# Attention and feed-forward on one core: the first two query blocks with queries on partitions, weights in half portions through a PSUM bank, and the opening's order in a table

## The chip, the cores and the metric

The kernel runs on one core of one Trainium2 chip. Five engines work side by side, each in the order of its own instructions, and wait for one another by semaphores: TensorE (PE, with its weight loads as PEld), VectorE (DVE), ScalarE (ACT), GpSimd (POOL) and SyncE (SP), which issues all transfers here. The metric is the device time of one execution in microseconds; lower is better.

## The reference

Block-causal attention of 8 batches with 8 heads, 576 positions and 64 features a head, then a feed-forward layer on the 4608 tokens. All of it is float32, and the feed-forward weights arrive as float64.

```python
scores = q @ k.T / sqrt(64)            # per batch and head
mask = (i // 64) >= (j // 64)          # a query block sees its own and earlier key blocks
attn = softmax(where(mask, scores, -1e9))
x = (attn @ v) laid out as [8 * 576, 512]
h = x @ w_in                           # 512 x 2048
out = (h * sigmoid(h)) @ w_out         # 2048 x 512
```

## The kernel before

**Tokens.** The queries of a head are treated in three ways. The first 64 (they see 64 keys) are done by `First`, four batches at a time, groups `a` and `b`. The second 64 (they see 128 keys) are done by `Second`, two batches at a time, groups `c1[0]` to `c1[3]`. The other 448 are done by `Unit`, one head at a time, 64 units in a loop. The feed-forward works on blocks of 256 tokens: blocks 0 and 1 are the tokens of `First`, blocks 2 and 3 those of `Second`, and 14 more come from the units.

**Products.** A *step* of a block covers two tiles of 128 hidden features. It has two products with `w_in` (`ffn1`, 12 matmuls each, L514) and, two steps later (`LAG`), two with `w_out` (`ffn2`, 6 matmuls each, L538). Between them stand `silu` (ScalarE, L521) and `split_g` (upper part on ScalarE, L526; lower part on GpSimd, L527). All operands are split in two float32r parts, whose products are added up. `ffn(n)` issues n products; there are 576 in all. Block 0 keeps its output in bank 2 and in the bank `U`, which the units need, so block 0 must be finished before the unit loop begins: 57 products are issued ahead of it. `EVEN` says how many steps blocks 0 and 1 take by turns. In the loop, `AHEAD` (152) is the number of products that are due when unit 17 starts; `pace` spreads them.

**Weights.** `Weights` turns float64 words into float32 in SBUF, 16 portions of two halves: `rebias` (ScalarE, L117), three bit steps on VectorE (L126, L130, L134), `his` (upper part, ScalarE, L144), `los` (lower part, GpSimd, L148). `weigh(k)` treats a whole portion, and its bit steps alternate between the halves. They read and write SBUF only.

**First and Second.** The scores stand with keys on partitions. A maximum over keys is therefore a 32-by-32 transposing reduction (`ttr`, L153), four copies (L454), four reductions and a transposing broadcast (`bcast`, L157); the sums go the same way. One exponential covers a bank of 512 columns (L378, L463). The normalization follows the product with `v`, and the tokens are split by `split_x` (ScalarE, L324; GpSimd, L325).

**Order.** Each engine runs its instructions in the order in which the code below writes them (`manual_schedule`): the opening is written out by hand from L625 to L685, then comes the loop over units. Transfers wait in SP's one queue, in the same order.

Of the kernel before, what the change touches and what calls it, by code (L numbers as in the profile page):

```python
# [56 lines left out]
def attn_ffn(ctx: ExitStack, tc: tile.TileContext, qk, v, qk0, v0, qk1, v1, w_in, w_out, out):  # L57
# [29 lines left out]
    class Weights:  # L87
        """Two ff tiles of w_in, or of w_out, in two halves."""

        def __init__(u, kind, d, raw, work):  # L90
            u.kind, u.d, u.tags, u.wtags = kind, d, raw, work
            if kind == "in":
                u.parts = [[w[:, 2 * i : 2 * i + 2, d * 256 : d * 256 + 256] for w in wi] for i in range(2)]
            else:
                u.parts = [[w[:, 2 * d + i, :] for w in wo] for i in range(2)]

        def load(u):
            """The float64 words."""
            u.raw = [
                T[:, :1024].bitcast(I64) if t == "T" else sp.tile([P, 512], I64, tag=t, name="wst", bufs=2 if t == "g2" else 1)  # L100
                for t in u.tags
            ]
            for i, st in enumerate(u.raw):
                if u.kind == "in":
                    src = w_in[2 * i * P : (2 * i + 2) * P, u.d * 256 : u.d * 256 + 256]
                    nc.sync.dma_start(out=st.rearrange("p (c f) -> p c f", c=2), in_=src.rearrange("(c p) f -> p c f", p=P))
                else:
                    f = 2 * u.d + i
                    nc.sync.dma_start(out=st, in_=w_out[f * P : f * P + P, :])
# [4 lines left out]
        def rebias(u):
            u.w = [sp.tile([P, 512], F32, tag=t, name="wm", bufs=2 if t == "ot" else 1) for t in u.wtags]
            for i in range(2):
                nc.scalar.activation(u.w[i], u.word(i, 1).bitcast(F32), AF.Copy, scale=REBIAS)  # L117

        def bits(u):
            """float32's bits, an instruction a step: exponent and upper fraction, sign, lower fraction.  # L120
            What lies under 2**-119 stays under it."""
            a = [z.bitcast(U32) for z in u.w]
            first = u.kind == "in" and u.d == 0  # its halves come one after the other
            for i, j in [(0, 0), (0, 1), (1, 0), (0, 2), (1, 1), (1, 2)] if first else [(i, j) for j in range(3) for i in range(2)]:
                if j == 0:
                    nc.vector.tensor_scalar(  # L126
                        out=a[i], in0=a[i], scalar1=3, scalar2=0x7FFFFFF8, op0=ALU.logical_shift_left, op1=ALU.bitwise_and
                    )
                elif j == 1:
                    nc.vector.scalar_tensor_tensor(  # L130
                        out=a[i], in0=u.word(i, 1), scalar=0x80000000, in1=a[i], op0=ALU.bitwise_and, op1=ALU.bitwise_or
                    )
                else:
                    nc.vector.scalar_tensor_tensor(  # L134
                        out=a[i], in0=u.word(i, 0), scalar=29, in1=a[i], op0=ALU.logical_shift_right, op1=ALU.bitwise_or
                    )
                yield
# [4 lines left out]
        def his(u):
            for i in range(2):
                nc.scalar.copy(u.parts[i][0], u.shaped(i))  # L144

        def los(u):
            for i in range(2):
                nc.gpsimd.tensor_tensor(out=u.parts[i][1], in0=u.shaped(i), in1=u.parts[i][0], op=ALU.subtract)  # L148

# [616 lines left out]
```

## Time and profile before

| | us |
|---|---|
| median of 3 runs | 1109.41 (1109.28 to 1111.64) |
| span of the profiled execution | 1107.8 |
| PE busy | 1047.5 (95%) |
| VectorE busy | 843.4 (76%) |
| ScalarE busy | 760.3 (69%) |
| GpSimd busy | 776.2 (70%) |

The span is the time from the first to the last instruction of the one execution that was profiled; its busy times are shares of that span over stages with different limits, so they say little by themselves. A row of the profile's groups reads: line, engine, operation, output and inputs by the program's names, shapes, count, then busy time, mean ns of one, and the idle time of the engine just before them with what ended it. The cut that matters here is by stage: the opening up to the loop's first scores, the first 17 units, and the rest.

### The profile page before, as it was taken

What the parts mean: (1) busy time and instruction counts of PE and PEld (TensorE: products, weight loads), DVE (VectorE), ACT (ScalarE), POOL (GpSimd) and SP (SyncE); (2) the same over time, 40 slices, a digit from 0 to 9 for tenths busy, and PEclk for the clock granted to TensorE, in tenths of its full rate; (3) what the DMA queues carried; (4) which work ended last, traced back from release to release, by engine and by line L of the source; (5) the groups of instructions that cost most, each with busy time, mean ns of one, the idle gap of its engine ahead of it and who ended that gap; (6) DMA issues with size and microseconds to landing.
All of it is one profiled execution on the core that took longest, in us unless ns stands there. A gap on an engine that the chain in (4) does not pass through costs nothing.

```text
span 1107.8 us, 19852 instructions
## 1 busy us (share of the span) xinstructions
PE 1047.5 (95%) x6848; PEld 941.5 (85%) x6848; DVE 843.4 (76%) x2504; ACT 760.3 (69%) x1222; POOL 776.2 (70%) x758
## 2 busy tenths in 40 slices
PE   4696789999999999999999999999999999999998
PEld 3585677888898999898999999999999898989997
DVE  6999995899999988888888888888888888810000
ACT  2454655888888787878787878778886878742221
POOL 1466558788888877878787878787787888642221
PEclk9798899999999999999999999999999999999999
DMA  7256522323223222212122212122322212000000
GB/s 247 91 172 186 156 88 64 91 54 79 66 68 78 56 69 71 70 51 70 51 71 68 76 51 70 51 71 59 76 60 51 70 51 79 23 20 20 1 20 19
DMA packets 44067, 79.92 MB, mean 72 GB/s; under 512 B 9152, under 2 KB 23488, under 8 KB 43968
## 3 DMA queue, kind: packets, MB, share of 16 engines
q1 hardware_dynamic: 43968, 78.66, 25.7%
q8 instruction: 54, 0.88, 0.4%
q14 instruction: 45, 0.37, 0.1%
HBM read 69.21 MB, written 9.44 MB: 71 GB/s over the span
## 4 chain that ended last, share of the span: by engine, by line
PE 69%; DVE 21%; ACT 3%; issue 3%; DMA 2%; POOL 1%; SPq 0%; POOLq 0%; DVEq 0%; ACTq 0%
PE o L538 28%; PE h L514 28%; PE U L294 6%; PE S L216 6%; DVE wm L130 2%; DVE Mx L153 2%; DVE Dx L153 2%; DVE wm L134 1%; DMA qk<-in_qk_dram 1%; DVE Xm L163 1%; DVE m L230 1%; DVE T L247 1%; DVE mb L157 1%; DVE X L482 1%; DVE Xd L163 1%
## 5 line engine op out<-in xcount | busy, mean ns | idle before, releaser
L514 PE MATMUL h<-x,wi 128*128 128x256 f32 x3456 | 448.9, 284 | 14.3 <-ACT x L324 11.8
L514 PEld LDWEIGHTS h<-x,wi 128*128 128x128 f32 x3456 | 432.3, 190 | 26.9 <-ACT x L324 12.1
L538 PE MATMUL o<-wo,g 128*128 128x512 f32 x1680 | 431.4, 401 | 2.1 <-ACT ot L545 2.1
L538 PEld LDWEIGHTS o<-wo,g 128*128 128x128 f32 x1680 | 305.2, 190 | 66.8 <-ACT ot L545 4.0
L267 POOL TENSOR_TENSOR pl<-p,ph 128x448 fp32r<-128x448 f32 (+1 forms) x192 | 225.5, 1204 | 107.8 <-ACT ph L260 107.8
L527 POOL TENSOR_TENSOR g<-g,g 128x512 fp32r<-128x512 f32 x144 | 186.8, 1297 | 115.7 <-ACT g L526 111.9
L153 DVE TRANSPOSE_TENSOR_REDUCE Mx<-S 64x4 f32<-64x128 f32 (+4 forms) x384 | 129.9, 401 | 94.8 <-PE S L216 94.6
L521 ACT ACTIVATE g<-h 128x512 f32<-128x512 f32 x144 | 86.0, 597 | 97.4 <-POOL g L527 56.1
L153 DVE TRANSPOSE_TENSOR_REDUCE Dx<-p 128x14 f32<-128x448 f32 (+3 forms) x320 | 123.3, 448 | 0.3 <-ACT p L255 0.3
L526 ACT CAST g<-g 128x512 fp32r<-128x512 f32 x144 | 89.4, 621 | 47.2 <-PE o L538 44.8
L193 POOL TENSOR_TENSOR qh<-qkraw,qh 64x576 fp32r<-64x576 f32 x64 | 101.4, 1584 | 6.8 <-ACT qh L189 2.1
L255 ACT ACTIVATE p<-T 128x512 f32<-128x512 f32 (+1 forms) x192 | 103.7, 603 | 0.7
L260 ACT CAST ph<-p 128x512 fp32r<-128x512 f32 (+1 forms) x192 | 101.9, 594 | 0.0
L294 PE MATMUL U<-ph,vc 128*128 128x448 f32 (+3 forms) x320 | 92.9, 303 | 1.7 <-ACT g L521 0.9
L216 PE MATMUL S<-qh 128*128 128x448 f32 (+3 forms) x320 | 92.7, 302 | 0.1
L521 ACT ACT_TABLE_LOAD x69 | 88.5, 1283 | 1.2
L255 ACT ACT_TABLE_LOAD x64 | 82.1, 1283 | 3.2 <-DVE T L245 2.0
L216 PE MATMUL S<-ql,qh 128*128 128x448 f32 (+3 forms) x320 | 84.0, 307 | 0.0
L294 PE MATMUL U<-pl,vc 128*128 128x448 f32 (+2 forms) x256 | 79.4, 332 | 0.5 <-POOL pl L267 0.5
L195 POOL TENSOR_TENSOR ql<-qkraw,qh 128x448 fp32r<-128x448 f32 x64 | 74.4, 1163 | 5.0
L247 DVE TENSOR_TENSOR T<-S,mb 128x256 f32<-128x256 f32 (+2 forms) x192 | 73.4, 409 | 0.0
L189 ACT CAST qh<-qkraw 128x1024 fp32r<-128x1024 f32 x64 | 66.9, 1046 | 3.8 <-DMA qkraw<-in_qk_dram 2.5
(89 smaller groups left out, 1229.7 us busy)
## 6 DMA issues: line engine op xcount, KB each, us to landing
qkraw<-in_qk_dram SPq DMA_DIRECT2D x128, 256.0 KB, 3.8
vraw<-in_v_dram SPq DMA_DIRECT2D x64, 160.0 KB, 2.7
wst<-in_moe_w_in_dram SPq DMA_DIRECT2D x15, 512.0 KB, 4.9
out_dram<-ot SPq DMA_DIRECT2D x24, 256.0 KB, 3.5
wst<-in_moe_w_out_dram SPq DMA_DIRECT2D x11, 512.0 KB, 3.7
qk<-in_qk_dram SPq DMA_DIRECT2D x16, 256.0 KB, 5.5
v<-in_v_dram SPq DMA_DIRECT2D x12, 256.0 KB, 4.8
out_dram<-ot SPq DMA_DIRECT2D x24, 128.0 KB, 3.2
```

What stands on the lines that cost most here:

```text
L153: nc.vector.tensor_reduce(out=out, in_=in_, axis=AX.X, op=op, apply_transpose=True)
L193: nc.gpsimd.tensor_tensor(out=u.qh[64:, NQ:], in0=u.raw[64:, NQ:], in1=u.qh[64:, NQ:], op=ALU.subtract)
L216: nc.tensor.matmul(u.ps(c, w, m), u.kk[:, j * P : j * P + m], qq[:, q0 : q0 + w], start=i == 0, stop=i == 1)
L255: nc.scalar.activation(u.p[:, c:e], T[:, c:e], AF.Exp, scale=SCALE)
L260: nc.scalar.copy(u.ph[:, c:e], u.p[:, c:e])
L267: nc.gpsimd.tensor_tensor(out=u.pl[:, c:e], in0=u.p[:, c:e], in1=u.ph[:, c:e], op=ALU.subtract)
L294: nc.tensor.matmul(U[:, q0 : q0 + w], u.vc[:, j, :], pp[:, c : c + w], start=n == 0, stop=n == 8)
L514: nc.tensor.matmul(h[:, f, :], wi[wt][:, c, w], x[:, xt, :], start=n == 0, stop=n == 3 * CT - 1)
L521: nc.scalar.activation(g, hs.pop((blk, d)), AF.Silu)
L526: nc.scalar.copy(g2[:, 0], g)
L527: nc.gpsimd.tensor_tensor(out=g2[:, 1], in0=g, in1=g2[:, 0], op=ALU.subtract)
L538: nc.tensor.matmul(o, g2[:, gt, f, tk], wo[wt][:, 2 * d + f, :], start=d == 0 and n == 0, stop=d == NSTEP - 1 and n == 5,)
```

## The change

**First and Second** now share a class `Early` and have the queries on partitions. The maximum is a plain reduction along the row (L360). Each head has its own exponential, in place in PSUM, with the negative maximum as bias and the row sum as second output (L369): eight of 64 columns, or four of 128. The weights are normalized before the product with `v` (`norm`, L377 to L380), turned by PE against an identity (`turn`, L386), copied back to SBUF (`back`, L389), and multiplied with `v`. Both parts of the tokens are made straight from PSUM, the upper on ScalarE, the lower on VectorE. A half of a `Second` group is one batch; both halves, and then the product with `v`, use bank 0 one after the other.

**Weights** come in 32 half portions, `w0` to `w31`, each with its own load. The first two bit steps write bank 1, and the third writes SBUF again (L152, L153, L156).

**The order** of the opening is a table of 350 entries: `a.`, `b.`, `c0.` to `c3.` and `w0.` to `w31.` with a method and a half, `ffn` (one product), `silu`, and `part` (`split_g`). The head before the loop has 61 products instead of 57, and `EVEN` is 6, with one step of block 0 ahead. The token tiles `x` become one tile with 16 parts. Units, loop and `AHEAD` stay as they were; the first unit is loaded behind the table.

```diff
-EVEN = 5
+EVEN = 6
+HEAD = 61
+ORDER = """
+a.load w0.load w1.load b.load a.load_v w0.rebias a.scores w2.load w3.load a.max:0 a.exp:0 a.max:1 w0.bits a.exp:1 b.scores w4.load
...
+b.norm:1 w3.rebias w3.bits ffn b.turn:0 w4.rebias
...
+w13.bits c1.turn:0 c1.back:0 w14.rebias ffn w12.hi w17.load c1.scores:1 c1.max:1 w13.hi c1.exp:1 ffn c2.load w12.lo w14.bits
...
+"""
-    xbuf = [cp.tile([P, 2, TB], F32R, name=f"x{i}") for i in range(NX)]
+    xbuf = cp.tile([P, NX, 2, TB], F32R, name="x")
...
         def bits(u):
+            w, a = u.w.bitcast(U32), bank(1).bitcast(U32)
+            nc.vector.tensor_scalar(out=a, in0=w, scalar1=3, scalar2=0x7FFFFFF8, op0=ALU.logical_shift_left, op1=ALU.bitwise_and)
+            nc.vector.scalar_tensor_tensor(
+                out=a, in0=u.word(1), scalar=0x80000000, in1=a, op0=ALU.bitwise_and, op1=ALU.bitwise_or
+            )
+            nc.vector.scalar_tensor_tensor(
+                out=w, in0=u.word(0), scalar=29, in1=a, op0=ALU.logical_shift_right, op1=ALU.bitwise_or
+            )
...
+    class Early:
+        def max(u, k):
+            n = 512 // u.KEYS
+            u.m[k] = sp.tile([P, 8], F32, tag=f"m{k}", name="m")[:, :n]
+            nc.vector.tensor_reduce(out=u.m[k], in_=u.ps[k].rearrange("p (h j) -> p h j", j=u.KEYS), axis=AX.X, op=ALU.max)
+            nc.vector.tensor_scalar(out=u.m[k], in0=u.m[k], scalar1=-SCALE, scalar2=None, op0=ALU.mult)
+        def exp(u, k):
...
+            for h in range(n):
+                nc.scalar.activation(
+                    heads[:, h], heads[:, h], AF.Exp, bias=u.m[k][:, h : h + 1], scale=SCALE, accum_out=u.rs[k][:, h : h + 1]
+                )
+        def norm(u, k):
...
+            nc.vector.tensor_scalar(out=u.rs[k], in0=u.rs[k], scalar1=1e-9, scalar2=None, op0=ALU.add)
+            nc.vector.reciprocal(out=rr, in_=u.rs[k])
...
+            nc.vector.tensor_tensor(out=out, in0=heads, in1=rr.unsqueeze(2).to_broadcast([P, n, u.KEYS]), op=ALU.mult)
+        def turn(u, k):
+            p = u.p[k]
+            for c in range(CT):
+                s = slice(P * c, P * c + P)
+                nc.tensor.transpose(u.ps[k][:, s], p[:, s], ident)
+        def back(u, k):
+            nc.scalar.copy(u.p[k], u.ps[k])
...
+    class Second(Early):
...
+        def scores(u, k):
...
+            u.ps[k] = bank(0)
...
+        def hi(u):
+            x = u.tiles(2 + u.g // 2, P)
+            u.xs = [x[:, :, i, P * (u.g % 2) : P * (u.g % 2) + P] for i in range(2)]
+            nc.scalar.copy(u.xs[0], u.x.rearrange("p (c q) -> p c q", c=CT))
+        def lo(u):
+            nc.vector.tensor_tensor(out=u.xs[1], in0=u.x.rearrange("p (c q) -> p c q", c=CT), in1=u.xs[0], op=ALU.subtract)
...
-    steps = [(blk, d) for d in range(EVEN) for blk in range(2)]
+    steps = [(0, 0)] + [z for d in range(EVEN) for z in ((0, d + 1), (1, d))]
...
+    for token in ORDER.split():
+        name, _, method = token.partition(".")
+        if method:
+            method, _, k = method.partition(":")
+            getattr(names[name], method)(*[int(k)] if k else [])
+        else:
+            do(name)
+    units[0].load()
+    units[0].load_v()
+    units[0].split_hi()
+    units[0].split_lo()
+    units[1].load()
+    ffn(HEAD - count[0])
...
-        pace = 6 if i == 0 else 7 if i == 1 or i >= 17 else (AHEAD - count[0]) // (17 - i)
+        pace = 7 if i >= 17 else (AHEAD - count[0]) // (17 - i)
```

Where instructions now stand on VectorE, at the second group of `Second` (its scores in banks `S_1140` and `S_1141`; `wm` is a weight half, `wst` and `T` its float64 words). Before:

```order
L454 COPY X_1207<-M_1204 32x32 x4
L457 TENSOR_REDUCE m_1212<-X_1207 32x32 x4
L157 STREAM_TRANSPOSE p_1217<-m_1212 128x512
L157 STREAM_TRANSPOSE p_1218<-m_1212 128x512
L462 TENSOR_TENSOR p_1217<-S_1140,p_1217 128x512
L462 TENSOR_TENSOR p_1218<-S_1141,p_1218 128x512
L126 TENSOR_SCALAR wm<-wm 128x512 x2
L130 SCALAR_TENSOR_TENSOR wm<-wst,wm 128x512
L130 SCALAR_TENSOR_TENSOR wm<-T,wm 128x512
L134 SCALAR_TENSOR_TENSOR wm<-wst,wm 128x512
L134 SCALAR_TENSOR_TENSOR wm<-T,wm 128x512
```

The same group with the change (its first half's scores are in `S_675`, the bit steps' bank is `S_717`):

```order
L360 TENSOR_REDUCE m<-S_675 128x4
L361 TENSOR_SCALAR m<-m 128x4
L152 TENSOR_SCALAR S_717<-wm 128x512
L153 SCALAR_TENSOR_TENSOR S_717<-wst,S_717 128x512
L156 SCALAR_TENSOR_TENSOR wm<-wst,S_717 128x512
L377 TENSOR_SCALAR rs<-rs 128x4
L378 RECIPROCAL rr<-rs 128x4
L380 TENSOR_TENSOR p_673<-S_675,rr 128x512
```

The six instructions of the fold stand no longer between scores and weights, and one half's three bit steps stand between the maximum and the normalization.

On ScalarE, from one group's exponentials to the next weights (`wi_73` and `wo_75` are the upper parts of the weights, `g` the hidden features). Before:

```order
L463 ACT_TABLE_LOAD
L463 ACTIVATE p_1217<-p_1217 128x512
L463 ACTIVATE p_1218<-p_1218 128x512
L117 ACTIVATE wm<-wst 128x512 x2
L144 CAST wo_75<-wm 128x512 x2
L521 ACT_TABLE_LOAD
L521 ACTIVATE g<-h 128x512
L526 CAST g_1320<-g 128x512
L495 COPY p_1218<-S_1293 128x512
L324 CAST x_94<-p_1217 128x128
```

With the change:

```order
L369 ACT_TABLE_LOAD
L369 ACTIVATE S_675,rs<-S_675,m 128x128 x4
L533 ACT_TABLE_LOAD
L533 ACTIVATE g<-h 128x512
L538 CAST g_759<-g 128x512
L389 COPY p_673<-S_675 128x512
L146 ACTIVATE wm<-wst 128x512
L164 CAST wo_75<-wm 128x512 x2
L369 ACT_TABLE_LOAD
L369 ACTIVATE S_793,rs<-S_793,m 128x128 x4
```

A group's two exponentials under one table load become two sets of four, each with its own load, and the copy back of the first half stands ahead of the second half's.

More of the change, by code (lines that the diff above doesn't have):

```diff
@@ L43 @@
 HALVES = [(448, 320, 128, 128, 2, 3), (960, 448, 0, 384, 1, 4)]
+ORDER = """
+a.load w0.load w1.load b.load a.load_v w0.rebias a.scores w2.load w3.load a.max:0 a.exp:0 a.max:1 w0.bits a.exp:1 b.scores w4.load
+w1.rebias a.norm:0 w5.load a.norm:1 w1.bits a.turn:0 w0.hi b.max:1 w2.rebias a.back:0 a.turn:1 a.back:1 b.max:0 a.pv w1.hi a.hi:0
+w1.lo w0.lo a.hi:1 a.lo:0 b.exp:0 a.lo:1 w2.bits b.exp:1 b.norm:0 b.load_v ffn b.norm:1 w3.rebias w3.bits ffn b.turn:0 w4.rebias
+w6.load b.turn:1 c0.load w2.hi b.back:0 b.back:1 b.pv w3.hi w3.lo c0.scores:0 w7.load w2.lo silu w5.rebias w6.rebias b.hi:0
@@ new lines @@
+w4.bits ffn w5.bits w8.load b.lo:0 part b.hi:1 ffn b.lo:1 w4.hi c0.max:0 w5.hi silu w6.bits w4.lo ffn c0.exp:0 w8.rebias w7.rebias
+w9.load c0.norm:0 c0.load_v w10.load w7.bits ffn w5.lo w6.hi part c0.turn:0 c0.back:0 w6.lo c0.scores:1 c0.max:1 w11.load w7.hi
+w9.rebias w7.lo w8.bits w12.load c0.exp:1 w10.rebias c0.norm:1 silu ffn w8.hi w9.bits w8.lo ffn ffn c1.load c0.turn:1 c0.back:1
+w11.rebias w10.bits w9.hi ffn c0.pv w9.lo part c0.hi w10.hi w10.lo c0.lo silu w13.load ffn ffn c1.scores:0 w12.rebias ffn w14.load
@@ new lines @@
+w11.bits c1.max:0 w11.hi c1.load_v w15.load part w12.bits w13.rebias w11.lo c1.exp:0 ffn ffn w16.load ffn silu part c1.norm:0
+w13.bits c1.turn:0 c1.back:0 w14.rebias ffn w12.hi w17.load c1.scores:1 c1.max:1 w13.hi c1.exp:1 ffn c2.load w12.lo w14.bits
+w14.hi w13.lo ffn c1.norm:1 w15.rebias w14.lo ffn ffn w15.bits silu c1.turn:1 c1.back:1 ffn w16.rebias w18.load w19.load w15.hi
+w16.bits w20.load w15.lo c1.pv ffn part w18.rebias w17.rebias c1.hi c1.lo w19.rebias c2.scores:0 w16.hi c2.load_v ffn w17.bits
@@ new lines @@
+w16.lo c2.max:0 silu w17.hi w17.lo ffn ffn w21.load ffn ffn w18.bits part w22.load c2.exp:0 c2.norm:0 silu w18.hi w19.bits
+w23.load c2.turn:0 part w18.lo c2.back:0 w20.rebias ffn w21.rebias c2.scores:1 c2.max:1 c2.exp:1 ffn w20.bits w19.hi ffn silu
+w19.lo ffn c2.norm:1 part w21.bits w24.load c3.load ffn w20.hi c2.turn:1 ffn c2.back:1 w25.load w21.hi w20.lo w23.rebias
+w22.rebias w21.lo c2.pv c2.hi w22.bits w24.rebias silu w26.load ffn c2.lo ffn c3.scores:0 ffn c3.load_v w22.hi w23.bits w25.rebias
@@ new lines @@
+part c3.max:0 w23.hi w24.bits w27.load ffn silu c3.exp:0 ffn w28.load w25.bits w23.lo c3.norm:0 w24.hi w25.hi w22.lo w24.lo ffn
+w29.load part w26.rebias ffn c3.turn:0 ffn w26.bits w25.lo c3.back:0 c3.scores:1 c3.max:1 w27.rebias ffn w29.rebias c3.exp:1 silu
+c3.norm:1 w27.bits w26.hi ffn ffn w30.load c3.turn:1 ffn w31.load w28.rebias w27.hi ffn w26.lo c3.back:1 part w28.bits ffn
+w29.bits w28.hi silu c3.pv c3.hi w30.rebias c3.lo w27.lo ffn w28.lo w29.hi w29.lo ffn part w30.bits ffn silu ffn part w30.hi
@@ L46, in blocks32 @@
+w30.lo w31.rebias w31.bits ffn ffn w31.hi ffn silu ffn w31.lo part
+"""
 def blocks32(ap):
@@ L94, in __init__ @@
             else:
-                u.parts = [[w[:, 2 * d + i, :] for w in wo] for i in range(2)]
+                u.parts = [w[:, 2 * d + i, :] for w in wo]
         def load(u):
[L99 to L109, printed above, removed]
@@ L119, in bits @@
         def bits(u):
[L122 to L137, printed above, removed]
@@ new lines, in bits, with shaped @@
+            nc.vector.scalar_tensor_tensor(
[4 more added lines that the diff above has]
+            )
+        def shaped(u):
+            return u.w.rearrange("p (c f) -> p c f", c=2) if u.kind == "in" else u.w
+        def hi(u):
+            nc.scalar.copy(u.parts[0], u.shaped())
@@ L151, in ttr @@
+        def lo(u):
+            nc.gpsimd.tensor_tensor(out=u.parts[1], in0=u.shaped(), in1=u.parts[0], op=ALU.subtract)
+            ready.add((u.kind, u.d, u.i))
     def ttr(out, in_, op):
@@ L380, in pv @@
-        def pv(u):
-            U = [pU.tile([P, 512], F32, tag="U", name="U"), bank(2)] if u.g == 0 else [bank(0), bank(1)]
-            u.U = [z.rearrange("p (k c q) -> p k c q", k=2, c=4) for z in U]
-            for k in range(2):
-                for h in range(H):
-                    for i, a in enumerate(HALF):
-                        s = slice(64 * h, 64 * h + 64)
-                        nc.tensor.matmul(u.U[i][HALF[h % 2], k, h // 2], u.v[k][a, s], u.p[a, 512 * k + 64 * h : 512 * k + 64 * h + 64], start=True, stop=True)
@@ new lines, in out, with pv @@
+        def out(u, n):
+            return u.all[:, :, n]
+        def pv(u):
+            for k in range(2):
+                for c in range(CT):
+                    for e, b in enumerate(HALF):
+                        for n, a in enumerate(HALF):
+                            h = 64 * (2 * c + e)
+                            s, t = 256 * k + 64 * c, 128 * c + 64 * e
+                            nc.tensor.matmul(u.ps[n][b, s : s + 64], u.v[k][a, h : h + 64], u.p[k][a, t : t + 64], start=True, stop=True)
@@ new lines, in hi, with lo, __init__, load @@
+        def hi(u, n):
+            if n == 0:
+                u.x = u.tiles(u.g, TB).rearrange("p c i (k n q) -> p i n k c q", k=2, n=2)
+            nc.scalar.copy(u.x[:, 0, n], u.ps[n].rearrange("p (k c q) -> p k c q", k=2, c=CT))
+        def lo(u, n):
+            src, x = u.ps[n].rearrange("p (k c q) -> p k c q", k=2, c=CT), u.x
+            nc.vector.tensor_tensor(out=x[:, 1, n], in0=src, in1=x[:, 0, n], op=ALU.subtract)
+    class Second(Early):
+        KEYS = 128
+        def __init__(u, g):
+            u.g, u.m, u.rs = g, {}, {}
+        def load(u):
+            u.qk = [sp.tile([P, 1024], F32, tag=t, name="qk1")[:, : CT * 3 * D] for t in ("qkraw", "qh")]
+            for k in range(2):
+                nc.sync.dma_start(out=u.qk[k], in_=qk1[2 * u.g + k])
@@ L536, in ffn2 @@
         for f in range(2):
+            assert ("out", d, f) in ready
             for gt, wt in ((0, 0), (0, 1), (1, 0)):
@@ L723, in attn_ffn @@
         ffn(3)
-    for _ in pieces:
-        pass
+    ffn(10000)
 _INS = ["qk", "v", "qk0", "v0", "qk1", "v1", "moe_w_in", "moe_w_out"]
```

350 lines of the change are left out of this document (107 added, 243 removed).

## The prediction

> **What bounds the kernel now.** I read the page first: its span, and the strips of 40 slices (27.7 us each; a digit is the busy share in tenths).
>
> ```profile
> span 1107.8 us, 19852 instructions
> ...
> PE   4696789999999999999999999999999999999998
> ...
> DVE  6999995899999988888888888888888888810000
> ...
> PEclk9798899999999999999999999999999999999999
> ```
>
> From the seventh slice on TensorE (PE) is full to the end. Only the first six slices leave it room, and there VectorE (DVE) is the full engine. Next the stages, cut at the first feed-forward product (25.7), where a regular rhythm begins (57.9), at the first scores of the unit loop (175.6), and at units 2 and 17 of that loop. Columns: stage, its length, then busy time of PE, weight loads, DVE, ScalarE (ACT), GpSimd (POOL), then the clock granted to PE.
>
> ```profile
> 0.00:25.70 25.70, 9.61 (x192) 8.72 (x192) 15.53 (x36) 6.74 (x11) 3.46 (x8) 0.95 0.79 266
> 25.70:57.90 32.20, 20.99 (x149) 17.44 (x149) 29.58 (x51) 14.46 (x27) 15.01 (x15) 0.72 0.24 84
> 57.90:175.60 117.70, 92.89 (x638) 81.41 (x637) 108.66 (x179) 63.71 (x110) 75.87 (x76) 0.90 0.46 140
> 175.60:203.20 27.60, 27.60 (x177) 24.96 (x176) 19.74 (x69) 21.33 (x33) 19.08 (x22) 1.00 0.40 107
> 203.20:370.90 167.70, 164.63 (x1031) 145.61 (x1031) 161.64 (x526) 144.65 (x229) 147.48 (x144) 1.00 0.28 69
> 370.90:1107.80 736.90, 731.79 (x4670) 663.34 (x4668) 508.20 (x1646) 509.45 (x817) 515.26 (x496) 1.00 0.20 53
> ```
>
> PE's idle time is 16.1 + 11.2 + 24.8 = 52.1 us before the loop and 8.2 after it. So a change of the opening can win at most some 50 us, and it wins by bringing the loop's first scores forward from 175.6. Who PE waits for in the opening (total, times, longest):
>
> ```profile
> PE S L471 <- ACT p L463: 18.0, 4, 6.6
> PE h L514 <- ACT x L324: 11.8, 2, 6.0
> ```
>
> Both are attention chains of the first two query blocks, and behind both stands DVE: 108.66 of 117.70 us busy between 57.9 and 175.6. Its rows in the opening (mean ns of one after the bar's busy time):
>
> ```profile
> L130 DVE SCALAR_TENSOR_TENSOR wm<-wst,wm 128x512 uint32<-128x512 uint32 x26 | 25.8, 1018 | 0.0
> L126 DVE TENSOR_SCALAR wm<-wm 128x512 uint32<-128x512 uint32 x32 | 25.0, 817 | 4.3 <-ACT wm L117 4.3
> L148 POOL TENSOR_TENSOR wi<-wm,wi 128x512 fp32r<-128x512 f32 x16 | 21.9, 1391 | 23.4 <-ACT wi L144 23.4
> ...
> L134 DVE SCALAR_TENSOR_TENSOR wm<-wst,wm 128x512 uint32<-128x512 uint32 x26 | 21.3, 846 | 0.0
> ...
> L462 DVE TENSOR_TENSOR p<-S,p 128x512 f32<-128x512 f32 x8 | 5.0, 664 | 0.0
> ...
> L130 DVE SCALAR_TENSOR_TENSOR wm<-T,wm 128x512 uint32<-128x512 uint32 x6 | 4.1, 683 | 0.0
> ...
> L169 DVE RECIPROCAL rr<-rs 128x16 f32<-128x16 f32 x4 | 1.0, 253 | 0.1
> ```
>
> The three bit steps of a half portion take 0.82 + 1.02 + 0.85 = 2.68 us, 80 us for 32 halves. The same step on the same shape takes 1.02 us in one group and 0.68 in the other: a third of it is not work.
>
> **The change, part by part.** *Bit steps.* The intermediate goes through a PSUM bank, so no step has two SBUF inputs. I price the first step by L462 (0.66, a PSUM operand) and the others by L130's faster group (0.68): 2.02 us a half. Bounds: 2.68 if nothing is freed, and nothing below 2 x 0.66 for the two that were at 0.68.
> The Trainium skill's page "SBUF — State Buffer" (the engine side and its shared port pair) says that a VectorE instruction with two SBUF inputs and a GpSimd instruction take the port pair in turn, for its whole length. By that rule the new steps run at 2.02; without it at 2.68. The two L130 groups agree with it, but they do not prove it.
>
> *Attention on DVE and POOL.* The 32-by-32 folds go: per group of two batches the eight `L454`/`L482` copies, eight small reductions, four transposes. A half now has one reduction (0.66), a small scaling, two small steps of the normalization and one multiply (0.66). With 0.25 for a small step (L169) that is 2.1 us, and the split's lower part (0.66) once a group: 4.9 us. POOL loses all splits of these tokens; it keeps 32 weights at 1.39 and 15 lower parts of `g`, 65 us, and cannot bound.
>
> *ScalarE.* It gains: a head pair's exponentials become 4 instructions of 128 columns per half (8 of 64 in the first block), each waiting for the one before, plus a copy back from PSUM.
>
> ```profile
> L117 ACT ACTIVATE wm<-wst 128x512 f32<-128x512 f32 x26 | 17.0, 675 | 16.1 <-DMA wst<-in_moe_w_in_dram 11.6 <-POOL wo L148 2.0 <-DMA wst<-in_moe_w_out_dram 1.4
> ...
> L144 ACT CAST wi<-wm 128x512 fp32r<-128x512 f32 x16 | 9.9, 620 | 11.3 <-DVE wm L134 11.3
> ...
> L521 ACT ACTIVATE g<-h 128x512 f32<-128x512 f32 x15 | 8.9, 594 | 2.1 <-POOL g L527 2.0
> ...
> L526 ACT CAST g<-g 128x512 fp32r<-128x512 f32 x14 | 8.7, 619 | 0.7 <-PE o L538 0.4
> ...
> L521 ACT ACT_TABLE_LOAD x5 | 6.4, 1283 | 0.1
> ...
> L463 ACT ACT_TABLE_LOAD x4 | 5.1, 1283 | 16.4 <-DVE p L462 16.3
> ...
> L463 ACT ACTIVATE p<-p 128x512 f32<-128x512 f32 x8 | 4.7, 624 | 3.7 <-DVE p L462 3.7
> ...
> L324 ACT CAST x<-p 128x128 fp32r<-128x128 f32 x16 | 3.6, 296 | 13.7 <-POOL p L497 13.7
> ...
> L324 ACT CAST x<-xs 128x256 fp32r<-128x256 f32 x8 | 2.7, 403 | 7.9 <-DVE xs L411 7.9
> ...
> L495 ACT COPY p<-S 128x512 f32<-128x512 f32 x4 | 2.3, 578 | 0.0
> ```
>
> L324 gives 0.30 us at 128 columns and 0.40 at 256, so 0.24 at 64. No row shows an exponential with a pointer bias and a row sum. Bounds: 0.24 and 0.30 from below, 0.62 (L463, 512 columns) from above; I take 0.30 and 0.40, near the short rows. Table loads go from 10 (these nine and the program's first) to 14 in the opening.
>
> *PE.* Prices from its order of time (start, length):
>
> ```profile
> 57.90 2.98 PE L514 MATMUL h<-x,wi 128*128 128x256 f32 x24
> 60.72 2.96 PE L538 MATMUL o<-wo,g 128*128 128x512 f32 x12
> 63.52 2.99 PE L514 MATMUL h<-x,wi 128*128 128x256 f32 x24
> ...
> 70.91 1.95 PE L446 MATMUL S<-qk 128*128 128x128 f32 x16
> 72.61 3.07 PE L514 MATMUL h<-x,wi 128*128 128x256 f32 x24
> ...
> 155.92 1.21 PE L471 MATMUL S<-p,v 128*64 128x64 f32 x32 [1.58 <-ACT p L463]
> 157.06 1.67 PE L538 MATMUL o<-wo,g 128*128 128x512 f32 x6
> ```
>
> Two products start 2.82 and 2.80 us apart: 1.41 each. Scores of a group take 1.70 for eight 128-column matmuls, its products with v 1.14. The new eight turns (128 columns too) are priced 1.70: a group is 4.5 us. Bounds for the turns: 0 if hidden among other work, 3.4 if each costs double.
>
> *To the first product.* Before:
>
> ```profile
> 8.34 1.12 PE L358 MATMUL S<-qk 64*64 64x64 f32 x16 [0.77 <-DMA qk<-in_qk_dram]
> ...
> 25.74 0.58 PE L514 MATMUL h<-x,wi 128*128 128x256 f32 x1 [5.76 <-ACT x L324]
> ```
>
> The scores again end near 9 (same bytes, half the transfers). Then maximum 0.9, two times eight exponentials 4.8, normalization 1.2, turn 0.85, two copies back 1.2, products with v 1.8, three split steps 1.9, and some ten handshakes of 0.1: 22.7. The second four batches follow on ScalarE: 4.8 of exponentials after the first split (21.2), normalization, turn, copies, products 5.2, five other ScalarE instructions 3.8 that the table puts ahead, the split 1.9: their tokens stand near 36, when four products are done.
>
> *From 36 to the loop.* The table gives each of the four groups of the second block a stretch; ScalarE's instructions in it, with the prices above (weights in / weights out / silu / upper part / exponentials / PSUM copies / loads):
> first: 5, 6, 2, 2, 8, 3, 2 = 3.4 + 3.7 + 1.2 + 1.2 + 3.2 + 1.7 + 2.6 = 17.0 us; PE there 6 products and 3.7, 12.2.
> second: 7, 6, 3, 3, 8, 3, 4 = 22.1; PE 12 products, 21.4.
> third: 5, 6, 3, 3, 8, 3, 4 = 20.8; PE 21.4.
> fourth: 6, 7, 4, 3, 8, 3, 2 = 20.1; PE 14 products, 24.2.
> DVE in the second: six halves at 2.02 and 4.9, 17.0. The larger ones sum to 17.0 + 22.1 + 21.4 + 24.2 = 84.7. Thirteen products to the new head of 61 follow: 18.3. 36 + 84.7 + 18.3 = 139.0.
> Queues between: each of eight halves now passes scores, maximum, exponential, normalization, turn and copy through one bank, 6 us alone, with 3 to 5 products (4.2 to 7 us) beside it. I add 1 us a half: **147**. Bounds: 133.8 (PE alone, 57 products and 17.4), and 175 if each half costs the 4.5 us that one group costs now (18.0 in 4).
>
> *In the loop.* Four products moved ahead of it: three fewer in units 0 and 1, where PE is busy 27.60 of 27.60 (at most 4.2 us), one fewer to unit 17, where DVE is busy 161.64 of 167.70. Unit 0's values reach their split hardly sooner, so I take 3.0 + 0.5 = 3.5; bounds 0 and 5.6. The counts agree again at unit 17, and nothing behind it moves.
>
> The sum: 175.6 - 147 + 3.5 = 32.1 us off the profiled span of 1107.8. The runs' median, 1109.41, lies 1.6 above that span, and I keep that: **1077**.
>
> **The rivals.** *ScalarE stalls at table switches.* If every load held ScalarE 1.4 us longer than its row, the four stretches would grow to 19.8, 27.6, 26.3 and 25.6 (ScalarE, beside PE's 24.2): 99.3, and 1.4 more ahead of 36; the loop would start at 163, and the time be 1093. The case of before:
>
> ```profile
> 33.20 1.28 ACT L521 ACT_TABLE_LOAD   x1
> 34.50 0.60 ACT L521 ACTIVATE g<-h 128x512 f32<-128x512 f32 x1
> ```
>
> The next instruction starts 0.02 us after the load's end, so I give it 0.05. The Trainium skill's page "ScalarE: Activation LUTs" (What ACT_TABLE_LOAD costs) gives each switch a drain of about 1.38 us behind the 1.28, which would be this rival; the two rows disagree with it.
>
> *The bank frees nothing.* If the bit steps stay at 2.68, DVE has 21.0 us in the second stretch, nearly ScalarE's 22.1, and each half's chain queues a further 1.2 us: start at 157, 1087. Chance 0.10.
>
> *Slower: the chain through one bank.* PE works in order; if each half's chain (0.85 scores, 0.9 maximum, 1.3 load, 1.6 exponentials, 1.2 normalization, 0.85 turn, 0.6 copy: 7.3) is not covered, because bits, weights and loads stand ahead of its steps in their queues, PE waits. From 5.0 us a half on (40 us over 139.0) the gain is gone; at the longest wait shown, 6.6, eight halves cost 53 us, the start is 192, the time 1122. For it: L471's wait. Against: that wait stood behind a DVE that was full. Chance 0.06.
>
> **How the numbers follow.** Forecast 0.70, between 1064 (PE alone) and 1088; bank 0.10; switches 0.05; waits in between, 1093 to 1111, 0.07, of which 0.02 within 0.2% (about what a measurement can tell from no change); slower 0.06; below 1064 0.02. Range 1064 to 1093, which holds 0.85. Faster 0.92, same 0.02, slower 0.06.
>
> **What would show it.** Right: the first scores of the loop near 147, PE's granted clock near 1 from 58 on, the three bit steps near 0.67 each with GpSimd busy, ScalarE the fullest engine in the second stretch. Wrong: small exponentials above 0.6, PE waits of several us before turns, bit steps still at 0.8 to 1.0, or a loop whose first 17 units take longer.

## The result and the profile after

| | before | with the change |
|---|---|---|
| median (runs), us | 1109.35 (1108.73 to 1111.64) | 1079.67 (1078.91 to 1079.9) |
| span of the profiled execution | 1107.8 | 1077.8 |
| first scores of the loop | 175.57 | 147.44 |
| unit 17 starts | 370.93 | 341.19 |

The ratio is 0.9729 [0.9715, 0.9743]: 2.7% faster. The change of the span is 30.0 us, where the prediction had 32.1. (A unit's start is its broadcast `mb`, L177, on VectorE.)

The page of the changed kernel, its span and three strips:

```profile
span 1077.8 us, 20036 instructions
...
PE   4799999999999999999999999999999999999998
...
DVE  5776749999998888888888888888888888800000
...
PEclk9899999999999999999999999999999999999999
```

PE is full from the third slice (54 us) on, before from the seventh, and its clock has one low digit instead of three. VectorE's row of nines is gone from the opening. By stage, cut at the first product (22.1), at 60.3, at the loop's first scores (147.4), at units 2 and 17 (columns as before: PE, weight loads, DVE, ACT, POOL, then PE's clock):

```profile
0.00:22.10 22.10, 8.85 (x200) 7.43 (x200) 10.76 (x21) 12.63 (x43) 3.40 (x10) 1.00 0.76 286
22.10:60.30 38.20, 31.32 (x281) 27.13 (x281) 29.31 (x51) 32.32 (x86) 15.16 (x12) 0.87 0.56 184
60.30:147.40 87.10, 82.78 (x646) 71.95 (x645) 54.90 (x93) 66.37 (x134) 44.62 (x35) 1.00 0.48 147
147.40:170.80 23.40, 23.40 (x153) 21.34 (x152) 19.73 (x68) 19.10 (x29) 18.32 (x20) 1.00 0.44 122
170.80:341.20 170.40, 165.59 (x1020) 145.72 (x1019) 161.53 (x527) 144.86 (x228) 147.05 (x145) 0.99 0.28 68
341.20:1077.80 736.60, 731.73 (x4670) 663.29 (x4668) 508.15 (x1646) 509.46 (x817) 515.25 (x496) 1.00 0.20 53
```

Idle time of PE ahead of the loop: 13.3 + 6.9 + 4.3 = 24.5 us, before 52.1. That is 27.6 of the 30.0 us. PE's busy time ahead of the loop hardly changes (122.95 us, before 123.49), though four products more are done in it; the granted clock is 0.87 and 1.00 in the second and third stage, where it was 0.72 and 0.90. In the third row VectorE is busy 54.90 of 87.10 us, where the comparable stage of before had 108.66 of 117.70. The stage from unit 17 on is the same within 0.3 us. One stage became longer: units 2 to 17, 170.4 us instead of 167.7.

What PE waits for up to 150 us (total, times, longest):

```profile
PE S L386 <- DVE p L380: 7.8, 4, 3.6
PE S L436 <- DMA qk<-in_qk_dram: 4.8, 2, 4.4
PE o L436 <- DMA qk<-in_qk_dram: 3.4, 2, 3.2
PE o L386 <- DVE T L380: 3.0, 1, 3.0
```

The waits of before, 18.0 us on the exponentials of L463 and 11.8 on the split tokens, are gone. In their place stands a new one, the turn (L386) that waits for the normalized weights (L380): 10.8 us in five waits, about a third of what went. Two of the five, 6.6 us, stand in the first block (before 16.29 and 30.08 us); the second block has three, 4.2 us. The transfers of the very first operands are not new: they open the program, with 8.2 us of waits now and 9.0 before.

VectorE's bit steps in the opening (mean ns of one after the bar's busy time):

```profile
L152 DVE TENSOR_SCALAR S<-wm 128x512 uint32<-128x512 uint32 x32 | 22.0, 687 | 10.4 <-ACT wm L146 9.9
L153 DVE SCALAR_TENSOR_TENSOR S<-wst,S 128x512 uint32<-128x512 uint32 x25 | 17.4, 696 | 0.9
L156 DVE SCALAR_TENSOR_TENSOR wm<-wst,S 128x512 uint32<-128x512 uint32 x25 | 17.2, 687 | 2.2
```

They take 0.69 + 0.70 + 0.69 = 2.07 us a half, against 2.68 before and 2.02 predicted. (The 2.68 holds for the 26 halves whose words lie in `wst`; the prediction's 80 us over all 32 halves are 2.51 each.) ScalarE's exponentials in the same part:

```profile
L369 ACT ACTIVATE S<-S,m 128x128 f32<-128x128 f32 x32 | 10.9, 342 | 2.8 <-DVE m L361 1.9
...
L369 ACT ACTIVATION_READ_ACCUMULATOR S<-S,m 128x1 f32 x40 | 7.7, 193 | 0.0
...
L369 ACT ACTIVATE o<-o,m 128x64 f32<-128x64 f32 x16 | 4.6, 289 | 0.5
```

One line of code is two instructions: the exponential, and a second one of 0.19 us that reads out the row sum. The time from one to the next is in the order of time, below.

### The profile page after: what moved, and what is told of

It reads as the page before. It is cut to its first block, busy times and chain, and to the rows that moved or that the text cites. A ratio compares the mean times of both kernels' runs of the same rounds, so it can differ in the third digit from the quotient of the medians.

```text
span 1077.8 us, 20036 instructions
## 1 busy us (share of the span) xinstructions
PE 1043.7 (97%) x6960; PEld 936.9 (87%) x6960; DVE 784.4 (73%) x2404; ACT 784.7 (73%) x1334; POOL 743.8 (69%) x716
## 4 chain that ended last, share of the span: by engine, by line
PE 84%; ACT 8%; DVE 4%; POOL 1%; issue 1%; DMA 1%; SPq 0%; ACTq 0%; POOLq 0%
PE h L526 34%; PE o L551 33%; PE U L314 7%; PE S L236 7%; ACT S L369 1%; POOL pl L287 1%; DVE Mx L173 1%; ACT p L275 1%; PE S L489 1%; ACT L275 1%; PE S L551 1%; ACT L533 1%; ACT L369 1%; ACT o L369 1%; ACT ph L280 1%
## 5 line engine op out<-in xcount | busy, mean ns | idle before, releaser
L551 PE MATMUL o<-wo,g 128*128 128x512 f32 x1680 | 427.1, 399 | 2.3 <-ACT ot L558 2.3
L533 ACT ACTIVATE g<-h 128x512 f32<-128x512 f32 x144 | 86.1, 598 | 99.3 <-POOL g L539 55.5
L236 PE MATMUL S<-qh 128*128 128x448 f32 (+3 forms) x320 | 92.7, 302 | 0.1
L344 ACT CAST x<-xu 128x256 fp32r<-128x256 f32 (+3 forms) x80 | 22.6, 339 | 71.0 <-DVE xu L329 71.0
```

Of the source, the lines that this page charges most:

```text
L236: nc.tensor.matmul(u.ps(c, w, m), u.kk[:, j * P : j * P + m], qq[:, q0 : q0 + w], start=i == 0, stop=i == 1)
L533: nc.scalar.activation(g, hs.pop((blk, d)), AF.Silu)
L551: nc.tensor.matmul(o, g2[:, gt, f, tk], wo[wt][:, 2 * d + f, :], start=d == 0 and n == 0, stop=d == NSTEP - 1 and n == 5,)
```

## The experiments

Ten kernels ran. Each ratio is to the kernel before.

**1. The bit steps in SBUF again, nothing else changed.**

```diff
-            w, a = u.w.bitcast(U32), bank(1).bitcast(U32)
+            w = a = u.w.bitcast(U32)
```

> The changed kernel (1079.7 us), with the intermediate of the three bit steps back in SBUF, in place; all else as changed. Theory: the bank takes the wait for GpSimd out of the bit steps (0.69 us each now, 0.82 to 1.02 before), but with the new order VectorE is busy only 54.9 of the 87.1 us before the loop, so it can take most of the 20 us back: bit steps return to 0.8 to 1.0, the loop's first scores move from 147 to 150 to 158, the time to 1083 to 1091. Rival A: the bank is what the opening was won by; then the scores move by the whole 20 us and the time is about 1100. Rival B: the bank frees nothing; the steps stay at 0.69 and the time at 1079.7.

Measured: 1086.34 us, ratio 0.9785 [0.9770, 0.9800]; the loop's first scores at 154.09. VectorE's groups in its opening:

```profile
L153 DVE SCALAR_TENSOR_TENSOR wm<-wst,wm 128x512 uint32<-128x512 uint32 x25 | 27.0, 1078 | 0.9
L156 DVE SCALAR_TENSOR_TENSOR wm<-wst,wm 128x512 uint32<-128x512 uint32 x25 | 25.2, 1008 | 0.9
L152 DVE TENSOR_SCALAR wm<-wm 128x512 uint32<-128x512 uint32 x32 | 19.2, 601 | 7.9 <-ACT wm L146 7.9
```

0.60 + 1.08 + 1.01 = 2.69 us a half. The gain of the bank sits in the two steps with two inputs; the step with one input is in the mean shorter in SBUF. These means mix two values, as the order of time shows, with GpSimd's row beside it:

```profile
38.53 2.80 POOL L167 TENSOR_TENSOR wo<-wm,wo 128x512 fp32r<-128x512 f32 x2
```

```profile
39.77 0.41 DVE L152 TENSOR_SCALAR wm<-wm 128x512 uint32<-128x512 uint32 x1
40.21 1.66 DVE L153 SCALAR_TENSOR_TENSOR wm<-wst,wm 128x512 uint32<-128x512 uint32 x1
41.91 0.69 DVE L156 SCALAR_TENSOR_TENSOR wm<-wst,wm 128x512 uint32<-128x512 uint32 x1
```

Of the 64 steps with two SBUF inputs, 43 take 0.69 or 0.70 us and 21 take 1.64 to 1.77, with nothing between; all 21 overlap an instruction of GpSimd, and none that runs beside a resting GpSimd is slow. The step with one input takes 0.41 to 0.43 beside a resting GpSimd and up to 1.53 beside a working one. Through the bank all 96 steps take 0.68 to 0.70, whether GpSimd works or not. So a second SBUF input is not slow by itself: what the bank takes away is the meeting with GpSimd. GpSimd's lower parts (L167) go from 1.29 to 1.43 and 1.48 us in the mean, so both engines lose. The bank is worth 6.7 us of the 29.7. This is the rival "the bank frees nothing", priced at 2.68 a half and 1087; made on purpose, it gives 2.69 and 1086.3. The two values agree with the rule of the Trainium skill's page "SBUF — State Buffer" (SBUF: two separate sides) that the shared port pair is held for a whole instruction.

**2. The bank alone, in the kernel before.** Its bit steps run half after half, through bank 1.

```diff
-            for i, j in [(0, 0), (0, 1), (1, 0), (0, 2), (1, 1), (1, 2)] if first else [(i, j) for j in range(3) for i in range(2)]:
...
+                for i in range(2):
+                    s = bank(1).bitcast(U32)
+                    u.bit(i, 0, a[i], None, s)
+                    yield
+                    u.bit(i, 1, None, s, s)
+                    yield
+                    u.bit(i, 2, None, s, a[i])
+                    yield
```

> The kernel before (1109.4 us), with only the bit steps through a PSUM bank (all halves but the first portion's, one half after the other); order, attention and transfers as before. Theory: there VectorE bounds the opening (108.7 of 117.7 us busy), so 30 halves at 2.06 instead of 2.68 give 10 to 19 us: 1090 to 1099, and VectorE stays the fullest engine. Rival A: the chains of the attention bound it, not VectorE's sum; then 0 to 5 us, 1104 to 1109. Rival B: bank 1 is shared with the scores and the products with v, and new waits for it make it slower than 1109.

Measured: 1107.12, ratio 0.9969 [0.9956, 0.9981]. VectorE was freed: each step 0.69 us (L140, L144, L148). But PE's waits in the opening are now:

```profile
PE S L459 <- ACT wi L157: 21.2, 3, 7.2
...
PE S L459 <- DVE wm L148: 5.1, 1, 5.1
```

The scores of the second query block (L459) use bank 1 too, and wait until the weights have left it: 26.3 us of waits where 18.0 stood before. So the theory failed: the time is rival A's, and its cause is the wait that rival B named. The bank frees VectorE here as well, but in the old layout it makes a new wait that takes nearly all of it back. That the new `Second` keeps to bank 0 would be what makes bank 1 usable; no run has the new `Second` in bank 1, so this is argued and not shown.

**3. Row sums on VectorE instead of ScalarE's second output.**

```diff
-                    heads[:, h], heads[:, h], AF.Exp, bias=u.m[k][:, h : h + 1], scale=SCALE, accum_out=u.rs[k][:, h : h + 1]
+                    heads[:, h], heads[:, h], AF.Exp, bias=u.m[k][:, h : h + 1], scale=SCALE
...
+            nc.vector.tensor_reduce(out=u.rs[k], in_=u.ps[k].rearrange("p (h j) -> p h j", j=u.KEYS), axis=AX.X, op=ALU.add)
```

> The changed kernel, with the row sums taken by VectorE (12 reductions of a bank, 0.69 us each) instead of as a second output of the 64 small exponentials, which the trace shows as a second ScalarE instruction of 0.19 us behind each. Theory: ScalarE is on the path only up to some 60 us (both chains of the first block: 16 exponentials in a row each), PE from there on (82.8 of 87.1 us busy). Then about 16 x 0.15 us less 0.7 of a reduction on each of two chains: 2 to 4 us earlier, 1076 to 1078. Rival: ScalarE bounds all of the opening; then some 9 us off ScalarE give 6 us or more, 1073 or less. Second rival: the reductions stand on the chain and give all of it back, 1079.7 or more.

Measured: 1080.7, ratio 0.9731 [0.9715, 0.9747]: no difference to the changed kernel. The first product comes earlier, at 20.75 instead of 22.11, and a product of the second stretch at 60.54 instead of 63.10, but the loop's first scores come at 149.34, 1.9 later. PE's largest wait is still the turn: 9.5 us in six waits, 10.8 in five before. In the first block, where ScalarE's chain is bare, taking the read-outs away gains; in the second it lengthens VectorE's part of a chain that PE waits for (run 7, with the first block's sums alone, has the gain without the loss). ScalarE as a sum does not bound the opening.

**4. The old pace, six and seven products in units 0 and 1.**

```diff
-        pace = 7 if i >= 17 else (AHEAD - count[0]) // (17 - i)
+        pace = 6 if i == 0 else 7 if i == 1 or i >= 17 else (AHEAD - count[0]) // (17 - i)
```

> The changed kernel, with six and seven products in units 0 and 1 as before (five and five as changed); HEAD stays 61, AHEAD 152, so units 2 to 16 have three products fewer. Theory: units 0 and 1 are bound by PE and take 23 us again (18.9 as changed, +4.2); units 2 to 16 are bound by VectorE, and three products fewer make them no shorter, but a TensorE clock of 0.5 over 2.8 us at unit 6 (the trace of the changed kernel) costs 2 us there, which may come or go. So 1081.5 to 1084. Rival: each product costs PE its 1.41 us wherever it stands; then the two stretches cancel and the time stays 1079.7.

Measured: 1080.8, ratio 0.9737 [0.9722, 0.9751]. Units 0 and 1 take 23.13 us instead of 18.87, as three products should; units 2 to 17 take 167.80 instead of 170.38, as before the change. Net, the start of unit 17 is 1.7 later. The two stages go as the theory had them; the time lies 0.7 under its range and can't be told from the changed kernel's. Units 2 to 17 have no drop of the clock here (see runs 9 and 10).

**5. Four products more ahead of unit 17.**

```diff
-AHEAD = 152
+AHEAD = 156
```

> The changed kernel (1079.7 us) with AHEAD 156 instead of 152: four more products are due by unit 17. Theory: units 2 to 16 are bound by VectorE (161.5 of 170.4 us busy) and leave PE 4.8 us idle, and one clock dip of 2 us; four products fit there, and the end of the kernel, where PE alone is busy, has four fewer: 3 to 6 us off, 1074 to 1077. Rival: PE and VectorE take turns as the bound there, every product costs its 1.41 us, and the time stays at 1079.7.

Measured: 1091.67, ratio 0.9831 [0.9817, 0.9846]. Units 2 to 17 take 170.67 us, so the four products cost nothing there, as the theory had it. But the next unit takes 20.83 us, and one later (758.91 to 780.34) 21.43. PE's waits between 335 and 365, and the stretches behind the longer one:

```profile
PE h L526 <- ACT x L344: 3.9, 1, 3.9
PE h L526 <- POOL x L345: 1.9, 1, 1.9
```

```profile
341.00:346.00 5.00, 2.21 (x8) 1.92 (x9) 4.94 (x16) 0.75 (x3) 4.34 (x5) 0.55 0.14 22
346.00:351.00 5.00, 5.00 (x23) 4.34 (x22) 0.67 (x4) 0.64 (x2) 0.00 (x0) 0.77 0.33 88
```

The products ask for tokens of the second batch that are not there: 5.8 us of waits, then 5 us at a clock of 0.55 and 5 at 0.77, while the other engines stand still behind PE (ACT 0.64 us busy, POOL 0.00 in the last row). Theory and rival had both missed this wait. `AHEAD` is bound by the tokens.

**6. The new methods and the bank in the old hand-written order**, each group's steps in the places of the old ones, with 57 products ahead of the loop, `EVEN` 5 and the old pace. The core of the edit:

```diff
-    for token in ORDER.split():
-        name, _, method = token.partition(".")
...
+    for n in range(2):
+        a.norm(n)
+    for n in range(2):
+        a.turn(n)
+        a.back(n)
+    a.pv()
+    weigh(0)
...
```

> The new attention of the first two blocks and the bit steps through the bank, but in the order written by hand before (whole portions, 4 products behind the scores of a group, 3 and 1 in its second part; 57 products ahead of the loop, the old turns of blocks 0 and 1, the old pace). Where the old order has no counterpart, a half's chain is written out in one go, with a portion's weights between exponentials and normalization. Theory: the chain through one bank (maximum, exponentials, normalization, turn, copy, second half) stands in PE's way wherever no products lie beside it, and the table is what covers it: PE waits 5 to 9 us a group, the loop begins at 165 to 180, the time is 1098 to 1113. Rival: VectorE's relief (151 us of busy time before the loop, some 95 now) is the gain, and the order matters little; then 1080 to 1090.

Measured: 1129.4, ratio 1.0175 [1.0158, 1.0192], slower than before. The loop's first scores come at 192.43. The stretch from 60 to 188 us, PE's largest wait up to 190, and a product behind such a wait:

```profile
60.00:188.00 128.00, 92.40 (x681) 78.91 (x680) 62.86 (x110) 69.96 (x152) 44.21 (x35) 0.85 0.40 127
```

```profile
PE S L363 <- DVE p L357: 27.9, 5, 8.6
```

```profile
110.81 1.08 PE L363 MATMUL S<-ident,p 128*128 128x128 f32 x4 [5.24 <-DVE p L357]
...
114.47 4.52 PE L503 MATMUL h<-x,wi 128*128 128x256 f32 x24
```

No engine is full: VectorE 62.86 of 128 us, ScalarE 69.96, PE 92.40. The time goes into the chain of each half, one step after another through one bank, with PE waiting up to 8.6 us before a turn; and behind such a wait two products take 4.36 us (114.47 to the next at 118.83) instead of 2.82. This is the mechanism of the prediction's slower rival, and near its start of the loop, 192. The changed kernel has the same chain, and its table lays products and weights beside it. Order, head and pace together are worth 1129.4 - 1079.7 = 49.7 us against this one order by hand, more than the whole change; which of the three gives how much was not measured.

**7 and 8. The row sums on VectorE in the first block alone; and with `AHEAD` 156.**

```diff
+                    **({} if u.KEYS == D else {"accum_out": u.rs[k][:, h : h + 1]}),
...
+            if u.KEYS == D:
+                nc.vector.tensor_reduce(out=u.rs[k], in_=u.ps[k].rearrange("p (h j) -> p h j", j=u.KEYS), axis=AX.X, op=ALU.add)
```

> The changed kernel with the row sums of the first block alone on VectorE (four reductions; 32 small exponentials lose their second instruction), those of the second block as changed. With all sums on VectorE the first product came 1.4 us and the fifth some 3 us earlier, but the loop 2 us later. Theory: the first block's two chains are on the path, the gain there is real (2 to 3 us) and was lost by the reductions in the second block's chains: 1076.5 to 1078. Rival: a later bound (weights, transfers) takes the gain back whatever the second block does: 1079.5 to 1081.

> The first block's sums on VectorE and AHEAD 156 together. If the two gains are in different stages they add: 1072 to 1075. Rival: one of the two is nothing; then the time is that of the other alone.

Measured: run 7 1077.01, ratio 0.9694 [0.9680, 0.9709]; run 8 1088.96, ratio 0.9807 [0.9793, 0.9822]. In run 7 the first product comes at 20.96 and the loop's first scores at 144.10, 3.3 earlier, of which 1.5 are lost again: its units 2 to 17 take 171.86 us, with two long periods (12.59 and 13.17) where the changed kernel has one (13.22). Run 8 gains as much by the first edit and pays the 12 us of run 5.

**9 and 10. The same products, in other units.** Both are run 7 with 91 products up to unit 17; six instead of five stand in units 3 to 8 (run 9), or in units 0 to 5 (run 10), instead of in the last six.

```diff
-        pace = 7 if i >= 17 else (AHEAD - count[0]) // (17 - i)
+        pace = 7 if i >= 17 else 6 if 3 <= i <= 8 else 5
```

> This kernel is the one that makes the row sums of the first block on VectorE, with the same 91 products between the opening and unit 17, but those units that get six products instead of five are units 3 to 8 instead of the last six. Theory (the drop of the granted clock comes where PE has too little to do, in a unit with five products): with six products around unit 6 the drop to 0.50 does not appear there, the period of 12.6 to 13.2 us becomes 11.2, units 2 to 17 take 168 to 170 us instead of 171.9, and the time is 1073.5 to 1076. Rival (PE waits there for GpSimd's lower parts, which six products push no earlier): the long period stays near 13 or moves to one of the units that lost a product, units 2 to 17 stay at 171 to 173, and the time is 1076.5 to 1078.5.

> As the run before it, but units 0 to 5 get the six products. Theory (VectorE bounds units 2 to 16, PE the units 0 and 1): the two products more in units 0 and 1 cost 2.8 us there, and the drop at unit 6 is not cured, since units from 6 on have five: 1078 to 1081. Rival (any product more ahead of unit 6 leaves units with five products in which VectorE runs further ahead, so that the drop goes as it did with the old pace of six and seven): units 0 and 1 lose 2.8, units 2 to 17 gain 2.5, and the time stays within 1076 to 1078.

Measured: run 9 **1075.21**, ratio 0.9681 [0.9668, 0.9695]; run 10 1078.18, ratio 0.9706 [0.9693, 0.9719]. First a place at the start of unit 6 of the changed kernel and one at the start of its unit 10, then one in run 9, then units 2 to 17 of run 7 and of run 9 (PE's busy time first, its clock third from the end):

```profile
213.00:217.00 4.00, 2.46 (x9) 1.40 (x10) 3.85 (x14) 3.97 (x6) 3.85 (x5) 0.98 0.00 1
217.00:219.80 2.80, 2.80 (x14) 2.80 (x15) 2.76 (x12) 2.69 (x5) 2.72 (x3) 0.50 0.01 3
...
259.00:263.00 4.00, 2.41 (x12) 1.34 (x11) 3.85 (x14) 3.97 (x6) 3.50 (x4) 1.00 0.07 23
263.00:266.00 3.00, 3.00 (x19) 2.61 (x20) 2.97 (x12) 2.95 (x5) 2.85 (x4) 1.00 0.00 0
```

```profile
277.40:281.40 4.00, 2.31 (x11) 1.25 (x9) 3.85 (x14) 3.97 (x6) 3.60 (x4) 1.00 0.10 34
281.40:284.40 3.00, 3.00 (x19) 2.60 (x20) 2.97 (x11) 2.95 (x6) 2.85 (x4) 1.00 0.00 0
```

```profile
167.47:339.33 171.86, 166.83 (x1019) 147.01 (x1019) 162.24 (x526) 144.82 (x228) 146.87 (x145) 0.98 0.28 67
```

```profile
168.22:336.01 167.79, 163.54 (x1019) 143.94 (x1019) 162.39 (x526) 144.00 (x228) 146.55 (x144) 1.00 0.28 69
```

In these two executions the same 1019 matmuls take 4.1 us less in run 9, 3.3 of them as PE's busy time: the clock, not the work. In run 9 the longest period of a unit there is 11.78 us and no drop is left. In run 10 unit 8 takes 13.12 us, with the clock at 0.62 there: the drop moved from unit 6 to unit 8. Its units 0 and 1 take 21.71 us instead of 18.88, as two products should, and its units 2 to 17 take 169.77.

What the two runs do not show is that a unit with five products, or a gap of a given depth, brings the drop. The kernel before and run 4 have five products in unit 6 too, which takes 11.61 and 11.63 us there. In the changed kernel PE is busy 2.41 of 4.00 us at 259, as little as at 213, and keeps its clock; run 9 has two such gaps (2.31 of 4.00 us at 277.4 and at 322.2), and keeps it behind both. So the six products moved the gaps and did not close them. Why the clock drops behind one gap and not behind another stays open. That PE waits for GpSimd there, as run 9's rival said, is so in both.

Run 9's time and its units 2 to 17 lie where its theory had them, but for the reason above that does not confirm it. By the times, run 9 is 4.5 us faster than the changed kernel (0.9681 against 0.9729, intervals apart), of which run 7's edit alone gives 2.7. Between runs 7 and 9 the intervals overlap (0.9680 to 0.9709, 0.9668 to 0.9695), so what the place of the products is worth is not clear of noise. Run 10 stands 0.2 us from the border of its two expectations: units 0 and 1 lost what both said, units 2 to 17 gained 2.1 us on run 7 where the rival said 2.5, and the drop neither stayed at unit 6 nor went.

## Why the prediction was right

**The start of the loop.** Predicted 147, measured 147.44. Its parts: the first product at 22.11 (22.7), the last tokens of the first block at 37.7 (36), the four stretches, and the tail. The stretches, cut where each group's tokens are split (L508), and the tail:

```profile
37.80:56.80 19.00, 15.86 (x133) 13.82 (x131) 15.66 (x28) 15.83 (x36) 9.33 (x8) 0.91 0.66 219
56.80:81.10 24.30, 22.72 (x183) 18.88 (x182) 17.75 (x29) 20.95 (x42) 12.57 (x11) 1.00 0.61 199
81.10:104.30 23.20, 21.54 (x178) 18.53 (x178) 15.43 (x28) 20.45 (x42) 11.75 (x10) 1.00 0.59 193
104.30:130.00 25.70, 24.43 (x196) 21.12 (x197) 19.86 (x35) 18.86 (x41) 11.81 (x11) 1.00 0.54 158
130.00:147.40 17.40, 17.40 (x115) 15.73 (x114) 4.53 (x7) 8.54 (x15) 11.32 (x9) 1.00 0.15 27
```

The stretches last 92.2 us, predicted 84.7 + 8 = 92.7; the tail 17.4, predicted 18.3. The sum came out better than its terms. By the prediction's terms PE would be busy 12.2 + 21.4 + 21.4 + 24.2 = 79.2 of the 92.7 us and idle 13.5; it is busy 84.55 and idle 7.65. Most of the difference stands in the first stretch (15.86 against 12.2, at a clock of 0.91), and that the two errors cancel is luck. One reading was wrong: ScalarE was to be the fullest engine in the second stretch, and it is PE (22.72 against 20.95). ScalarE's 22.1 was added up from the means of rows, but its instructions overlap where they follow one another: a copy of 0.58 us starts at 77.30 and the next instruction at 77.76. So its sum came out smaller in spite of eight read-outs of row sums that it did not have. Two slips in the sums changed little: the terms up to the first block's last tokens add up to 36.9, not 36, and by its own terms the fourth stretch of the table-load rival would stay at PE's 24.2, not 25.6.

**The bit steps.** 2.07 us a half against 2.02; run 1 shows the other bound, 2.69, and its time.

**Small prices, off in both directions.** The exponentials:

```profile
39.98 1.28 ACT L369 ACT_TABLE_LOAD   x1
41.27 0.34 ACT L369 ACTIVATE S<-S,m 128x128 f32<-128x128 f32 x1
41.54 0.19 ACT L369 ACTIVATION_READ_ACCUMULATOR S<-S,m 128x1 f32 x1
41.76 0.34 ACT L369 ACTIVATE S<-S,m 128x128 f32<-128x128 f32 x1
```

They follow one another after 0.49 us (128 columns; 0.40 predicted), and after 0.44 (64 columns, 8.60 to 9.04; 0.30 predicted). The second instruction is the difference; without it, in run 3, eight and four of them take 0.31 and 0.35 each:

```profile
7.93 2.52 ACT L369 ACTIVATE S<-S,m 128x64 f32<-128x64 f32 x8
```

```profile
37.69 1.47 ACT L369 ACTIVATE S<-S,m 128x128 f32<-128x128 f32 x4
39.08 0.65 ACT L146 ACTIVATE wm<-wst 128x512 f32<-128x512 f32 x1
```

So the price of the exponential itself was right, and the read-out was left out of it. For the sixteen ahead of the first product that is 2.2 us too little; by luck the chain made it up with an earlier start, as the first exponential runs at 8.18, when the prediction still waited for scores. The turns, in PE's order of time:

```profile
52.76 0.60 PE L386 MATMUL S<-ident,p 128*128 128x128 f32 x4
53.11 1.66 PE L526 MATMUL h<-x,wi 128*128 128x256 f32 x12
```

Four take 0.35 us up to the next product, 0.09 each where 0.21 was priced.

**The loop.** This is the term that was mis-sized: 3.5 us predicted, 1.5 measured. Units 0 and 1 won 4.2 (23.05 to 18.87; 3.0 predicted), near the three products at 1.41. Units 2 to 17 were to win 0.5 and lost 2.65 (167.73 to 170.38). With the opening's 28.1 (28.6 predicted) and 0.4 elsewhere that makes the 30.0. The prediction took VectorE's 161.64 of 167.70 us as the only limit there, and put the clock of PE at nothing. Unit 6, in which the clock drops, takes 13.22 us where it took 11.61 before: 1.6 of the 2.65. Units 9 to 13 take 1.5 us more together, without a drop, and the others a little less; the cause of that stays open.

**The rivals.** Stalls behind table loads: the row above starts its exponential 0.01 us behind the load's end, as before. Nor is there a gap ahead of the loads: ScalarE's idle time before the seven of L533 is 0.1 us in total, and before the six of L369 3.2, nearly all of it a wait for VectorE's maximum. That goes against the drain of 1.38 us that the Trainium skill's page "ScalarE: Activation LUTs" (What ACT_TABLE_LOAD costs) adds to the load. The bank that frees nothing: excluded by L153 and L156, and reproduced by run 1. The chain through one bank: of the eight halves of the second block three make PE wait before their turn, 4.2 us in total and 2.4 at most; the longest wait before a turn, 3.6, is the first block's. Run 6 shows the chain without the table's cover, 1129. Of the signs of being wrong, PE's waits of several us before turns came in this small measure, and units 2 to 17 became longer, though the first 17 units together did not (189.25 us, before 190.78).

## What to carry to other kernels

A change of method and a change of order are two changes: here the new method without its order is some 20 us slower than the old kernel, because it trades busy engines for a longer chain, and only an order that lays other work beside each link turns the freed time into a gain. A PSUM bank for an intermediate kept VectorE's steps from meeting GpSimd (1.08 to 0.70 us in the mean; alone they take 0.69 either way), so it pays where both engines are at work; but look first at who else uses the bank. A sum of busy times can come out right by errors that cancel: check its terms one by one, and an engine's granted clock in every stage where it has gaps.
